# Four quadrants of the array for the state's products, smaller key loads, another order in the joins, and a new table of shifts

## The chip, the core and the metric

The kernel runs on one core of a Trainium2 chip. The time is that of one execution on the device in microseconds (us); of several executions the median is given. TensorE (PE in the rows) has two clock levels, 1.2 and 2.4 GHz; the column PEclk of the rows is the granted clock as a share of the full one.

## What is computed

A recurrent attention with a state that is corrected at each token (the delta rule), for 4 batches of 8 heads with 768 tokens and a head width of 48, and behind it two expert stages on the 3072 tokens of width 384:

```python
k_n = k / (norm(k) + 1e-06)
for t in range(768):
    y[:, :, t] = einsum('bhd,bhde->bhe', q[:, :, t], state)
    v_old = einsum('bhde,bhd->bhe', state, k_n[:, :, t])
    state += b[:, :, t] * einsum('bhd,bhe->bhde', k_n[:, :, t], v[:, :, t] - v_old)
x = y.transpose(0, 2, 1, 3).reshape(3072, 384)
x = ((x @ w1) * (x @ w2) @ w3) @ w_out            # 384 -> 1024 -> 1024 -> 384
lg = x @ phi                                       # 384 -> 32 slots (8 experts of 4)
d = exp(lg - lg.max(0)); d /= d.sum(0) + 1e-09     # softmax over the tokens
slot_out = relu((d.T @ x) @ w1e[e]) @ w2e[e]       # for each expert e
c = exp(lg - lg.max(1)); c /= c.sum(1) + 1e-09     # softmax over the slots
out = c @ slot_out
```

## The kernel before, in words

The tokens go in 24 steps n of 32 tokens. Two steps make a chunk c (12 of them), four steps one solve s (6 of them). Within 32 tokens the recurrence becomes a triangular system for each batch and head, so 32 systems of 32x32 for a step, and a solve inverts those of four steps at once on VectorE (DVE).

- **Keys and queries.** `load(p)` brings the pair p of steps from memory into one of four buffers `kl` (the fourth is called `hold`): rows 64 to 111 and rows 0 to 63, two DMAs on SyncE's queue (L245, L246). `g_step` (L428) multiplies keys with keys ("g", the system's matrix) and keys with queries ("p"); the four first steps do both apart, all later ones together (tiles `gp`). `g_evac` brings the results out: `dg` (L373) on DVE for the solve, `praw`, `kl` (L384, L393, L400, L408) on ScalarE (ACT), GpSimd (POOL) or DVE for the chain.
- **Solves.** `solve_steps(s)`: DVE transposes `dg` to `gl` (L454), normalises the keys by Newton steps on small tiles `sm` (L461 to L482), and eliminates in `xl` (L509, L512; for solve 0 L520, L523). Solves 0 and 1 do two halves of 16x16 and join them: `join` (L525 to L533) multiplies the halves into `xf`, transposes part of it to `xn` (L531) and the whole to `w` (L533), and `join2` (L535) makes the missing quarter on TensorE (`j`, L542, L550) and adds it to `w` (L552). The other solves end in `fin`: a product on POOL (L558) and the transpose to `w` (L560).
- **Chain.** `chain_steps(n)` is one step of the recurrence: `pre` (L585), `ks` (L599: state by keys), `vv` (L610: `w` by values, four copies to `sv`, L575), `yy` (L620: the step's output), at odd n `ss` (L630: keys by new values, added to the state in the two PSUM tiles `sacc`, and copied back), and `xt` (L642: transposes of the output for the next stage).
- **Expert stage.** For each chunk `prod` (L695, tiles `ab`; L699 and L704 bring them out) as three products of the high and low parts, `gtr` (L712), then logits and softmax pieces (L719 to L793), and a tail for the experts (to L1129). The weights are split into high and low parts at the start (`t_w`, `wsl`, `hold`: L290 to L307).

In `ss` each of the 4 batches has 48x48 products, with keys of 64 rows (two steps) for 8 heads. Batches 0 and 1 take rows 0 to 63 and columns 64 to 111 of the array, batches 2 and 3 rows 64 to 127 and columns 0 to 47: two quadrants. A first loop does batches 0 and 2 for all heads, into `sacc0`, a second one 1 and 3, into `sacc1`. The trace records each of these fp32 matmuls twice, 64 records for a chunk.

What sets the order: each step of the program is put into a list `events` with a time (`when`, or `spread` over a range), all in units of a chunk. The times are worked out from constants at the head of the file and, for each label, a number in the table SHIFT. The list is sorted by that time, and the steps issue their instructions in this order; a scheduler then moves instructions within each engine by its own estimate of when their inputs are ready. Each engine runs its own list in order. DMAs of SyncE's queue are in order too.

## Time and profile before

| | us |
|---|---|
| median of 3 executions | 643.93 |
| lowest, highest | 643.07, 649.51 |
| the profiled execution | 642.53 |
| its span in the trace | 640.7 |
| TensorE busy in the span | 548.9 (86%) |
| VectorE busy | 400.3 (62%) |
| ScalarE busy | 278.6 (43%) |
| GpSimd busy | 161.8 (25%) |

Around the span lie 1.8 us that no engine's instruction covers. Busy shares are means over stages with different limits, so the table alone does not tell which engine sets the end.

### The profile page before, as it was taken

The page shows a single profiled execution, that of the slowest core. Times are in us where ns is not written, and L with a number is a line of the kernel's source. Part 1 is how long each engine was busy: PE and PEld are TensorE (multiplying, and loading weights), DVE is VectorE, ACT ScalarE, POOL GpSimd, SP SyncE. Part 2 cuts the span into 40 slices and gives each one's busy share as a digit, 9 for nine tenths or more (in the row PEclk, how much of TensorE's full clock was granted, in tenths as well). Part 3 has the DMA queues.
Part 4 walks back from the last instruction along what each step waited for, and adds up shares of the span by engine and source line. Part 5 has one row for each costly group of instructions (what it writes and reads, how often), then busy time and mean ns, then how long its engine had stood idle before and what let it go on. Part 6 is the DMA issues. An engine that isn't in the chain of part 4 may idle for free.

```text
span 640.7 us, 25996 instructions
## 1 busy us (share of the span) xinstructions
PE 548.9 (86%) x11417; PEld 458.8 (72%) x11417; DVE 400.3 (62%) x1257; ACT 278.6 (43%) x704; POOL 161.8 (25%) x215
## 2 busy tenths in 40 slices
PE   5324546888899799899999999897999999999996
PEld 4323435887777688679888888786989899886464
DVE  3996899998667115994379826997982313134124
ACT  1515644245574436454444455343444454333023
POOL 0726858334254016232030113004010000000100
PEclk9999666598999989999999999999999999999997
DMA  9904234446843720310404030122344130788848
GB/s 205 332 4 146 81 83 144 130 130 204 254 151 129 164 70 17 87 45 18 105 7 96 9 90 30 38 61 63 106 145 155 63 108 2 268 274 318 344 160 265
DMA packets 36945, 81.72 MB, mean 128 GB/s; under 512 B 4352, under 2 KB 17792, under 8 KB 35584
## 3 DMA queue, kind: packets, MB, share of 16 engines
q1 hardware_dynamic: 36832, 80.07, 40.9%
q8 instruction: 89, 1.46, 1.0%
q14 instruction: 24, 0.20, 0.1%
HBM read 69.57 MB, written 10.49 MB: 125 GB/s over the span
## 4 chain that ended last, share of the span: by engine, by line
PE 55%; DVE 26%; issue 6%; DMA 5%; POOL 4%; ACT 3%; SPq 0%; DVEq 0%; POOLq 0%; ACTq 0%
PE ab L695 24%; DMA kl<-kq 4%; PE gp L712 3%; PE yp L620 3%; DVE xl L512 2%; PE vp L610 2%; DVE tmp L509 2%; PE sacc L630 2%; PE gp L428 2%; PE ks L599 2%; PE sacc L1119 2%; PE hp L1098 2%; DVE gl L454 2%; DVE xl L487 1%; PE lp L719 1%
## 5 line engine op out<-in xcount | busy, mean ns | idle before, releaser
L695 PE MATMUL ab<-xT,wsl 128*128 128x256 f32 x1728 | 247.1, 296 | 3.6 <-DVE gT L704 2.2
L695 PEld LDWEIGHTS ab<-xT,wsl 128*128 128x128 f32 x1728 | 221.8, 196 | 15.6 <-issue 6.3
L704 DVE TENSOR_TENSOR gT<-ab,bs 128x256 f32<-128x256 f32 x84 | 35.2, 422 | 87.3 <-ACT bs L699 79.0
L699 ACT COPY bs<-ab 128x256 f32<-128x256 f32 x96 | 35.7, 371 | 68.0 <-PE ab L695 66.3
L585 POOL TENSOR_TENSOR v<-v,nnT 128x384 f32<-128x384 f32 x24 | 21.4, 894 | 139.2 <-DMA v<-vt 57.0
L575 ACT COPY sv<-vp 32x384 f32<-32x384 f32 x96 | 45.1, 470 | 16.2 <-PE vp L610 14.5
L512 DVE TENSOR_TENSOR xl<-xl,tmp 128x84 f32<-128x84 f32 (+35 forms) x220 | 51.5, 266 | 0.7
L509 DVE TENSOR_TENSOR tmp<-xl 128x84 f32<-128x84 f32 (+35 forms) x220 | 49.6, 259 | 0.4
L428 PE MATMUL gp<-kl 48*32 48x64 f32 (+1 forms) x1024 | 35.7, 275 | 11.7 <-ACT kl L408 8.6
L299 POOL TENSOR_TENSOR hold<-hold 128x384 f32<-128x384 f32 (+1 forms) x32 | 32.7, 1025 | 47.9 <-DVE hold L296 23.0
L428 PEld LDWEIGHTS gp<-kl 48*32 48x32 f32 x1024 | 26.1, 121 | 17.8 <-ACT kl L408 8.9
L713 ACT COPY gtok<-gp 128x512 f32<-128x512 f32 x48 | 28.2, 588 | 17.2 <-PE gp L712 15.0
L393 POOL TENSOR_TENSOR kl<-praw,cs 64x256 f32<-64x256 f32 x28 | 25.3, 903 | 33.5 <-ACT praw L384 32.3
L620 PE MATMUL yp<-sv,kl 112*32 112x48 f32 (+2 forms) x1280 | 26.3, 215 | 7.6 <-ACT sv L575 7.6
L291 ACT ACTIVATE hold<-hold,cs 128x384 int32<-128x384 int32 (+1 forms) x32 | 18.7, 589 | 27.7 <-DVE hold L290 27.3
L408 ACT COPY kl<-gp 32x256 f32<-32x256 f32 x64 | 23.2, 363 | 15.0 <-DVE kl L393 11.8
L620 PEld LDWEIGHTS yp<-sv,kl 112*32 112x32 f32 (+2 forms) x1280 | 20.4, 115 | 12.2 <-issue 8.4
L610 PE MATMUL vp<-v,w 32*32 32x48 f32 x1536 | 25.3, 207 | 3.1 <-DVE mst L738 0.9
L646 DVE TENSOR_TENSOR xT<-xp,xT 128x384 fp32r<-128x384 f32 x24 | 13.3, 553 | 22.8 <-ACT xT L645 22.6
L610 PEld LDWEIGHTS vp<-v,w 32*32 32x32 f32 x1536 | 20.1, 107 | 10.2 <-issue 6.0
L712 PE MATMUL gp<-cs,gT 128*128 128x128 f32 x168 | 26.9, 279 | 0.0
L400 POOL TENSOR_TENSOR kl<-praw,cs 32x256 f32<-32x256 f32 x28 | 23.2, 828 | 7.7 <-ACT praw L384 4.8
(248 smaller groups left out, 980.6 us busy)
## 6 DMA issues: line engine op xcount, KB each, us to landing
hold<-w SPq DMA_DIRECT2D x16, 384.0 KB, 3.3
v<-vt SPq DMA_DIRECT2D x24, 192.0 KB, 2.7
kk<-kt SPq DMA_DIRECT2D x12, 384.0 KB, 6.7
unitg<-w1e SPq DMA_DIRECT2D x6, 768.0 KB, 5.7
kl<-kq SPq DMA_DIRECT2D x8, 512.0 KB, 6.8
kl<-kq SPq DMA_DIRECT2D x8, 384.0 KB, 4.6
gx<-w SPq DMA_DIRECT2D x4, 768.0 KB, 8.2
raw_w<-w SPq DMA_DIRECT2D x4, 768.0 KB, 8.8
```

The lines of the kernel that those rows point to most:

```text
L299: G.tensor_tensor(out=w, in0=m, in1=w, op=ALU.mult)
L428: T.matmul(gp[trow(n, b), h - hs[0]], lhsT=t[r, k[j], kc], rhs=t[r, slots, kc], start=True, stop=True)
L509: V.tensor_tensor(out=tmp[:, 0:n, lo:hi], in0=x[:, j + 1:32, j:j + 1].to_broadcast([128, n, hi - lo]), in1=x[:, j:j + 1, lo:hi].to_broadca ...
L512: V.tensor_tensor(out=x[:, j + 1:32, lo:hi], in0=x[:, j + 1:32, lo:hi], in1=tmp[:, 0:n, lo:hi], op=ALU.add)
L575: A.copy(o, i)
L610: T.matmul(p[o, h * D:(h + 1) * D], lhsT=w[o, 8 * n4 + h, :], rhs=r[o, h, :], start=True, stop=True, tile_position=(o.start, o.start))
L620: T.matmul(p[qrow(b), h * D:(h + 1) * D], lhsT=kl[r, (6, 0)[b // 2] if t2 else (4, 2)[b // 2], kcol(h, b)], rhs=sv[r, b, h * D:(h + 1) * D ...
L695: T.matmul(o, lhsT=w[:, m, k], rhs=x[:, k], start=(n == 0), stop=(n == 8))
L699: A.copy(bs, p[:, 256:512])
L704: V.tensor_tensor(out=gt, in0=p[:, 0:256], in1=bs, op=ALU.mult)
L712: T.transpose(p[:, t * 256 + i * 128:t * 256 + (i + 1) * 128], gt[:, t * 128:(t + 1) * 128], ident)
L713: A.copy(gk, p)
```

## The change

1. `ss` goes through the heads once and takes the batches 0, 2, 1, 3 of each. `arow(b)` gives batches 1 and 2 the other columns than before: all four quadrants of the array are used. The copies to `sv` read the rows of `arow`.
2. `load` brings 48 instead of 64 rows for the lower part, except in the first three pairs and pair 5. Rows 48 to 63 are zeros, and stay in the buffer.
3. In solves 0 and 1, POOL's memset of `xf` covers only the two quarters that no product writes, and `join` goes through the halves in the order (16:32), (0:16), each with its own transpose to half of `w`; the transpose to `xn` comes between the last product and the last transpose.
4. Sixteen constants of the order and the table SHIFT are new. It gets labels that it did not have, 'P0' among them (the "p" products of the first four steps), and loses others.

```diff
-DR = 0.3
+DR = 0.306
...
-TW0 = 0.05
-TW1 = 0.8
-CL = 1.0
+TW0 = 0.155
+TW1 = 0.63
+CL = 1.002
...
-GX = 3.912
+GX = 3.584
...
-SHIFT = {'w3': -0.198, ... 'solve4': 0.109, ... 'solve3': 0.122, ...}
+SHIFT = {'w3': -0.205, ... 'solve3': 0.168, ... 'solve2': 0.287, ... 'P0': -0.066, ...}
...
+    def arow(b):
+
+        return srow(b if b % 2 == 0 else 3 - b)
...
-            SP.dma_start(out=t[0:64, 0:4, :], in_=kq[p][0:64])
+
+            n = 64 if p < 3 or p == 5 else 48
+            SP.dma_start(out=t[0:n, 0:4, :], in_=kq[p][0:n])
...
-                G.memset(st["xf"], 0.0)
+                G.memset(st["xf"][:, 0:16, 16:32], 0.0)
+                G.memset(st["xf"][:, 16:32, 0:16], 0.0)
...
-            for r in (slice(0, 16), slice(16, 32)):
+            W[s] = w = px.tile([128, 32, 32], F32, tag="W", name=f"w{s}", bufs=2)
+            for r in (slice(16, 32), slice(0, 16)):
                 V.tensor_tensor(out=xf[:, r, r], in0=x[:, r, r], in1=d[:, r].unsqueeze(2).to_broadcast([128, 16, 16]),
                                 op=ALU.mult)
-            V.transpose(xn.rearrange("p u c -> p c u"), xf[:, :, 0:16].rearrange("p r c -> p c r"))
-            W[s] = w = px.tile([128, 32, 32], F32, tag="W", name=f"w{s}", bufs=2)
-            ends[s] = V.transpose(w[:, :, :].rearrange("p u i -> p i u"), xf)
+                if r.start == 0:
+                    V.transpose(xn.rearrange("p u c -> p c u"), xf[:, :, 0:16].rearrange("p r c -> p c r"))
+                ends[s] = V.transpose(w[:, :, r].rearrange("p u i -> p i u"), xf[:, r, :])
...
-            for h, b in [(h, b) for b2 in range(2) for h in range(H) for b in (b2, b2 + 2)]:
-                r = slice(64 * (b // 2), 64 * (b // 2) + 64)
-                T.matmul(sacc[b % 2][srow(b), h * D:(h + 1) * D], lhsT=k[r, b % 2, h, :],
-                         rhs=sv[r, b, h * D:(h + 1) * D], start=False, stop=(c == NCH - 2),
-                         skip_group_check=True, tile_position=(r.start, 64 - 64 * (b // 2)))
+            for h in range(H):
+                for b in (0, 2, 1, 3):
+
+                    r, o = slice(64 * (b // 2), 64 * (b // 2) + 64), arow(b)
+                    T.matmul(sacc[b % 2][o, h * D:(h + 1) * D], lhsT=k[r, b % 2, h, :],
+                             rhs=sv[r, b, h * D:(h + 1) * D], start=False, stop=(c == NCH - 2),
+                             skip_group_check=True, tile_position=(r.start, o.start))
             for b in (0, 2, 1, 3):
-                copy(n, b, sv[srow(b), b, :], sacc[b % 2][srow(b), 0:384])
+                copy(n, b, sv[srow(b), b, :], sacc[b % 2][arow(b), 0:384])
```

The list of TensorE at the program's start before; g0 to g3 are the "g" products of the first four steps, p0_0 and p0_4 the two halves of the first "p" product, p1_0 and p2_0 those of the next steps:

```order
L428 MATMUL g0_0_147<-kl0_111 32x32 x30
L428 MATMUL g1_0_181<-kl0_111 32x32 x30
L428 MATMUL g2_0_215<-kl1_112 32x32 x32
L428 MATMUL g3_0_249<-kl1_112 32x32 x32
L428 MATMUL p0_0_283<-kl0_111 32x96 x16
L428 MATMUL p0_4_309<-kl0_111 32x96 x16
L428 MATMUL p1_0_335<-kl0_111 32x32 x32
L428 MATMUL p2_0_375<-kl1_112 32x96 x16
```

The same place after the change:

```order
L434 MATMUL g0_0_147<-kl0_111 32x32 x30
L434 MATMUL g1_0_181<-kl0_111 32x32 x30
L434 MATMUL p0_0_215<-kl0_111 32x96 x16
L434 MATMUL g2_0_241<-kl1_112 32x32 x32
L434 MATMUL p0_4_275<-kl0_111 32x96 x16
L434 MATMUL p1_0_301<-kl0_111 32x32 x32
L434 MATMUL g3_0_341<-kl1_112 32x32 x32
L434 MATMUL p2_0_375<-kl1_112 32x96 x16
```

Three "p" products stand ahead of g3 now, one of them ahead of g2; the numbers of records are those of the products times two.

The list of DVE at the join of solve 0 before, from the two products into `xf` to the weights' conversion (`t_w`):

```order
L529 TENSOR_TENSOR xf0_493<-xl0_489,sm0_469 128x16x16 x2
L531 STREAM_TRANSPOSE sums_92<-xf0_493 128x16x32
L533 STREAM_TRANSPOSE w0_555<-xf0_493 128x32x32
L290 TENSOR_SCALAR t_w0_632<-gx_72 128x768
L290 TENSOR_SCALAR t_w1_643<-raw_w1_641 128x768
L292 SCALAR_TENSOR_TENSOR t_w0_632<-gx_72,t_w0_632 128x768
```

The same place after the change, where the first row of `w` is the half 0:16 and the second the half 16:32:

```order
L537 TENSOR_TENSOR xf0_493<-xl0_489,sm0_469 128x16x16 x2
L540 STREAM_TRANSPOSE sums_92<-xf0_493 128x16x32
L541 STREAM_TRANSPOSE w0_553<-xf0_493 128x16x32
L296 TENSOR_SCALAR t_w0_703<-gx_72 128x768
L296 TENSOR_SCALAR t_w1_714<-raw_w1_712 128x768
L541 STREAM_TRANSPOSE w0_553<-xf0_493 128x16x32
L298 SCALAR_TENSOR_TENSOR t_w0_703<-gx_72,t_w0_703 128x768
```

The whole transpose has become two, and two conversions stand between them; the half 16:32, which `join2` reads first, is the last.

The list of DVE at the end of solve 3 before; `hold` and `dg4` are the results of `gp` for the steps 18 and 19, `w3` is the solve's result:

```order
L393 TENSOR_TENSOR hold_114<-gp18_4_5732,cs_90 64x256
L509 TENSOR_TENSOR tmp3_5266<-xl3_5263 128x12
L373 TENSOR_TENSOR dg4_4967<-gp19_0_5779,cs_90 128x256
L400 TENSOR_TENSOR hold_114<-gp19_0_5779,cs_90 32x8x32 x4
L512 TENSOR_TENSOR xl3_5263<-xl3_5263,tmp3_5266 128x12
L704 TENSOR_TENSOR gT5_0_5777<-ab5_1_5912,bs5_1_5931 128x256
L737 TENSOR_REDUCE soft4_5969<-lm4_5873 128x1
L560 STREAM_TRANSPOSE w3_5636<-xf3_5634 128x32x32
L738 TENSOR_TENSOR mst_93<-soft4_5969,mst_93 128x1
L704 TENSOR_TENSOR gT5_2_6069<-ab5_2_6048,bs5_2_6067 128x256
```

The same place after the change:

```order
L519 TENSOR_TENSOR xl3_5231<-xl3_5231,tmp3_5234 128x12
L714 TENSOR_TENSOR gT5_2_5994<-ab5_2_5973,bs5_2_5992 128x256
L568 STREAM_TRANSPOSE w3_5652<-xf3_5650 128x32x32
L747 TENSOR_REDUCE soft4_6004<-lm4_5934 128x1
L748 TENSOR_TENSOR mst_93<-soft4_6004,mst_93 128x1
L749 TENSOR_SCALAR soft4_6004<-mst_93 128x1
L714 TENSOR_TENSOR gT5_2_5994<-ab5_3_6065,bs5_3_6084 128x256
L760 SCALAR_TENSOR_TENSOR zst_94<-zst_94,soft4_6004 128x1
L379 TENSOR_TENSOR dg4_5008<-gp18_4_5796,cs_90 128x128
L399 TENSOR_TENSOR hold_114<-gp18_4_5796,cs_90 64x256 x2
L379 TENSOR_TENSOR dg4_5008<-gp19_0_5842,cs_90 128x256
L406 TENSOR_TENSOR hold_114<-gp19_0_5842,cs_90 32x8x32 x4
```

The evacuations of `gp` for steps 18 and 19 and the L737 (now L747) have moved behind `w3`; the two rows of gT around it have stayed in front.

The list of TensorE at `ss` of chunk 6 before, with the step's output `yp`:

```order
L630 MATMUL sacc0_109<-sv_108,kk6_5640 48x48 x3
L620 MATMUL yp13_6071<-sv_108,kl2_113 32x48 x2
L630 MATMUL sacc0_109<-sv_108,kk6_5640 48x48
L620 MATMUL yp13_6071<-sv_108,kl2_113 32x48 x29
L712 MATMUL gp5_0_6109<-cs_90,gT5_0_5777 128x128 x4
L630 MATMUL sacc0_109<-sv_108,kk6_5640 48x48 x12
L630 MATMUL sacc1_110<-sv_108,kk6_5640 48x48 x16
```

The list of TensorE at `ss` of chunk 9 after the change:

```order
L640 MATMUL sacc0_109<-sv_108,kk9_7617 48x48 x3
L628 MATMUL yp19_8135<-sv_108,hold_114 32x48 x2
L640 MATMUL sacc1_110<-sv_108,kk9_7617 48x48
L628 MATMUL yp19_8135<-sv_108,hold_114 32x48 x29
L640 MATMUL sacc1_110<-sv_108,kk9_7617 48x48
L640 MATMUL sacc0_109<-sv_108,kk9_7617 48x48
L640 MATMUL sacc1_110<-sv_108,kk9_7617 48x48 x2
L640 MATMUL sacc0_109<-sv_108,kk9_7617 48x48 x2
L640 MATMUL sacc1_110<-sv_108,kk9_7617 48x48 x2
```

And that at `ss` of chunk 6 after the change:

```order
L628 MATMUL yp13_6097<-sv_108,kl2_113 32x48
L640 MATMUL sacc0_109<-sv_108,kk6_5637 48x48 x11
L628 MATMUL yp13_6097<-sv_108,kl2_113 32x48 x2
L640 MATMUL sacc1_110<-sv_108,kk6_5637 48x48
L640 MATMUL sacc0_109<-sv_108,kk6_5637 48x48 x3
L628 MATMUL yp13_6097<-sv_108,kl2_113 32x48 x29
L640 MATMUL sacc1_110<-sv_108,kk6_5637 48x48 x13
L640 MATMUL sacc0_109<-sv_108,kk6_5637 48x48 x2
L640 MATMUL sacc1_110<-sv_108,kk6_5637 48x48 x2
```

In chunk 9 pairs for `sacc0` and `sacc1` alternate, as the code is written; in chunk 6 the scheduler has put most of one behind most of the other, so that pairs of two quadrants are next to each other again.

## Rows read from the trace of the kernel before

**Rows 1.** The page's busy time, share of the span and instructions of each engine.

```profile
PE 548.9 (86%) x11417; PEld 458.8 (72%) x11417; DVE 400.3 (62%) x1257; ACT 278.6 (43%) x704; POOL 161.8 (25%) x215
```

**Rows 2.** Busy time by stage: stretch, PE, PEld, DVE, ACT, POOL (instructions), PEclk, DMA share, GB/s.

```profile
0.00:41.00 41.00, 15.26 (x516) 12.04 (x516) 30.62 (x94) 11.31 (x33) 15.72 (x26) 1.00 0.74 211
41.00:102.50 61.50, 29.42 (x969) 24.68 (x970) 50.10 (x64) 32.03 (x64) 39.48 (x25) 0.76 0.27 81
102.50:155.00 52.50, 45.25 (x792) 39.94 (x791) 50.90 (x157) 19.98 (x46) 22.64 (x23) 0.76 0.53 165
...
318.00:366.00 48.00, 45.87 (x945) 40.04 (x944) 42.17 (x168) 21.32 (x55) 7.95 (x20) 1.00 0.17 39
...
436.70:588.00 151.30, 148.08 (x2732) 129.55 (x2732) 67.39 (x254) 65.19 (x168) 12.17 (x25) 1.00 0.44 149
```

**Rows 3.** Timeline of TensorE around `ss` of chunk 5: start, duration, instruction, count, idle before.

```profile
214.03 0.89 PE L620 MATMUL yp<-sv,kl 112*32 112x48 f32 x64
214.84 1.37 PE L630 MATMUL sacc<-sv,kk 64*48 64x48 f32 x52
```

**Rows 4.** DMA queues: packets of the instruction queue, MB, share of 16 engines.

```profile
q8 instruction: 89, 1.46, 1.0%
```

**Rows 5.** Busy time between two stalls of TensorE, columns as in rows 2.

```profile
13.50:22.80 9.30, 3.94 (x127) 3.46 (x127) 7.89 (x20) 3.94 (x12) 3.98 (x6) 1.00 1.03 269
```

**Rows 6.** Timeline of TensorE at the start.

```profile
13.53 0.70 PE L428 MATMUL g<-kl 48*32 48x32 f32 x35 [3.80 <-issue]
...
22.85 3.31 PE L428 MATMUL p<-kl 48*32 48x32 f32 x102 [4.50 <-issue]
```

**Rows 7.** Timeline of DVE: the last `dg` of solve 0.

```profile
14.33 0.42 DVE L373 TENSOR_TENSOR dg<-g,cs 128x256 f32<-128x256 f32 x1 [4.46 <-PE g L428]
```

**Rows 8.** Timeline of DVE in solve 0, two neighbouring pairs.

```profile
34.20 0.87 DVE L520 TENSOR_TENSOR sm<-xl 128x54 f32<-128x54 f32 x2
34.99 0.33 DVE L523 TENSOR_TENSOR xl<-xl,sm 128x54 f32<-128x54 f32 x2
```

**Rows 9.** Timeline of POOL beside them.

```profile
31.79 3.09 POOL L400 TENSOR_TENSOR kl<-praw,cs 32x256 f32<-32x256 f32 x4
```

**Rows 10.** Timeline of DVE: the transpose to `w` of solve 0.

```profile
39.22 1.87 DVE L533 STREAM_TRANSPOSE w<-xf 128x1024 f32<-128x1024 f32 x1
```

**Rows 11.** Timeline of TensorE: the first `j` of the join.

```profile
41.14 1.05 PE L542 MATMUL j<-w,dg 32*32 32x16 f32 x64 [10.98 <-DVE w L533]
```

**Rows 12.** DVE's L307 in 41 to 102.5: count, busy, mean ns, idle before it.

```profile
L307 DVE TENSOR_TENSOR wsl<-t_w,wsl 128x768 fp32r<-128x768 f32 x5 | 6.8, 1357 | 6.3 <-ACT wsl L306 6.3
```

**Rows 13.** Timeline of TensorE at 110.

```profile
113.77 0.61 PE L327 MATMUL wm<-phis,woT 128*128 128x32 f32 x2 [3.88 <-DVE sm L477]
```

**Rows 14.** Timeline of TensorE, 218 to 231.

```profile
218.40 2.40 PE L695 MATMUL ab<-xT,wsl 128*128 128x256 f32 x18
...
224.38 0.45 PE L550 MATMUL j<-t,sums 32*32 32x16 f32 x19 [2.99 <-issue]
...
226.22 4.19 PE L695 MATMUL ab<-xT,wsl 128*128 128x256 f32 x18
```

**Rows 15.** Busy time in 214.9 to 221.9 and 224.4 to 231, columns as in rows 2.

```profile
214.90:221.90 7.00, 5.99 (x188) 5.38 (x186) 0.98 (x2) 3.97 (x9) 0.83 (x1) 1.00 0.85 188
...
224.40:231.00 6.60, 6.60 (x144) 6.30 (x145) 0.51 (x2) 1.22 (x3) 0.00 (x0) 0.53 0.02 5
```

**Rows 16.** Timeline: where solve 3 begins and ends, and who takes its result.

```profile
318.09 1.98 DVE L454 STREAM_TRANSPOSE gl<-dg 128x1024 f32<-128x1024 f32 x1
```

**Rows 17.** The same, at the end of that solve.

```profile
363.89 2.00 DVE L560 STREAM_TRANSPOSE w<-xf 128x1024 f32<-128x1024 f32 x1 [1.38 <-POOL xf L558]
...
366.04 0.66 PE L610 MATMUL vp<-v,w 32*32 32x48 f32 x42 [0.87 <-DVE mst L738]
```

**Rows 18.** DVE by line in 318 to 366: the evacuations into `hold`.

```profile
L393 DVE TENSOR_TENSOR hold<-gp,cs 64x256 f32<-64x256 f32 x4 | 1.7, 416 | 0.1
```

**Rows 19.** DMA issues by line: count, KB each, us from issue to landing.

```profile
kl<-kq SPq DMA_DIRECT2D x8, 512.0 KB, 6.8
```

More of the change, by code (lines that the diff above doesn't have):

```diff
@@ L52 @@
 NL = 4
-J1 = (0.8, 1.2, 1.8, 2.0)
+J1 = (0.82, 1.107, 1.928, 1.875)
 NT12 = 2
@@ L57 @@
 NXT = 6
-GL = (0.35, 0.659, 0.85, 1.06)
+GL = (0.241, 0.657, 0.85, 1.123)
 NX = 6
 NO = 8
-GX = 3.912
+GX = 3.584
 LT = 1.799
-LTS = 0.311
+LTS = 0.351
 JAT = (1, 2, 3)
@@ L66 @@
 LAST = 1
-EA = 11.73
-JO = (-0.7, 0.1, 0.2)
-G1 = -0.341
-S1 = -0.015
-S2 = -0.01
+EA = 11.71
+JO = (-1.075, 0.115, 0.208)
+G1 = -0.294
+S1 = -0.004
+S2 = 0.013
 CA = 224
@@ L82 @@
 WM = (8, 8, 8, 8, 2, 2, 2)
-HT = 2.424
-L3 = -0.04
+HT = 2.423
+L3 = -0.057
 GA = (0.2, -0.09)
@@ L88 @@
 G2 = -0.017
-SA = -0.681
+SA = -0.74
 SB = -0.124
-SHIFT = {'w3': -0.198, 'load8': -0.01, 'solve4': 0.109, 'load6': -0.046, 'load9': -0.004, 'gtr3': 0.007, 'solve3': 0.122, 'prod11': 0.006, 'chain20': 0.021, 'gtr8': -0.158, 'chain17': -0.056, 'gtr6': 0.158, 'post0': -0.014, 'chain19': -0.018, 'gtr10': 0.016, 'back0': 0.257, 'gtr2': -0.016, 'chain13': -0.281, 'gtr9': 0.002, 'back1': 0.128, 'post10': 0.024, 'chain23': 0.001, 'gtr0': -0.012, 'G8': 0.031, 'gtr11': -0.005, 'chain8': 0.006, 'load5': -0.346, 'gtr5': -0.02, 'chain5': -0.257}
+SHIFT = {'w3': -0.205, 'load8': -0.01, 'load9': 0.015, 'solve3': 0.168, 'chain20': 0.021, 'gtr8': 0.095, 'chain17': -0.023, 'gtr6': 0.149, 'chain19': -0.039, 'gtr10': 0.066, 'back0': 0.296, 'chain13': -0.281, 'gtr9': 0.041, 'back1': 0.139, 'post10': 0.105, 'chain23': 0.001, 'gtr0': -0.012, 'G8': 0.031, 'gtr11': -0.005, 'chain8': 0.006, 'load5': -0.346, 'chain5': -0.257, 'prod2': 0.044, 'G18': 0.021, 'chain10': -0.112, 'load11': -0.054, 'gtr4': -0.02, 'post7': -0.027, 'prod3': 0.087, 'load4': -0.057, 'prod5': -0.13, 'post9': 0.119, 'chain11': -0.054, 'chain9': 0.065, 'post2': 0.098, 'chain12': -0.072, 'gtr3': 0.111, 'gtr1': 0.067, 'G4': -0.021, 'back4': -0.073, 'chain16': 0.013, 'gtr5': -0.036, 'chain15': -0.041, 'solve2': 0.287, 'prod8': 0.015, 'back5': -0.061, 'gtr2': -0.045, 'P0': -0.066, 'post1': 0.014, 'G14': -0.037, 'load6': -0.01, 'post11': 0.481, 'prod1': 0.019}
 TRACE = None
```

## The prediction

> **What bounds the kernel now.** I read the busy shares first [rows 1], then the busy time by stage [rows 2], because the mean of 86% for TensorE hides four different limits, and then in each stage the longest idle times of TensorE with what ended them. What the reader is to see:
> - 0 to 41 us: TensorE has 15.26 us of work in 41, DVE 30.62. The chain goes keys, "g" products, `dg`, solve 0 on DVE, `w`.
> - 41 to 155: DVE has 50.10 of 61.50 and then 50.90 of 52.50 (solves and weight conversions). TensorE is also at a mean clock of 0.76.
> - 318 to 366 (and the two like it, before 291.5 and 436.7): TensorE looks full, with 45.87 of 48.00, but it waits at the end for `w`; DVE's chain of solve 3 runs from `gl` at 318.09 [rows 16] to `w` at 363.89 plus 2.00, and `vp` follows at 366.04 after an idle 0.87 [rows 17]. What the trace puts beside that wait (mst) is a neighbour in DVE's list; `w` is the input.
> - 436.7 to 588: 148.08 of 151.30. TensorE is the bound.
>
> So what TensorE saves counts after 436.7 and, in part, in 155 to 318; before 155 and inside solves DVE's order counts.
>
> **The change, part by part.** All is reckoned against the profiled execution, 642.53 us, 1.4 below the median of the runs shown.
>
> *Quadrants.* 52 records of `ss` last 1.37 us, and the last begins some 0.2 before that ends: (1.37 - 0.20) / 51 = 23 ns each. The `yp` just before, which spreads over four column strips, takes (0.89 - 0.20) / 63 = 11 ns each [rows 3]. If four quadrants overlap as four strips do, a chunk saves 64 x 12 ns = 0.77. No row shows two products on the same columns at once, so the bounds are 0 and 11 x 0.77 = 8.5. I take 11 ns, the nearest row. But the new order, shown above, alternates fully only in seven of eleven chunks (2, 4, 5, 7 to 10, roughly); in chunk 6 pairs of two quadrants stand together as before, in 0 too, in 1 and 3 partly. Chunks 5 and 7 lie where `w` is awaited. That leaves chunks 2, 4, 8, 9, 10 whole, 5 x 0.77 = 3.9, and 0.4 of the rest: **-4.3**. The copies begin no later: both accumulators are done at the end of a run half as long, when `sacc0` was done before.
>
> The Trainium skill ("TensorE: Matmul & The Clock Gate", Part 3, "The mechanism") says that a weight load overlaps running products only where its group of rows differs. In the new order every second pair has the same rows as the pair before it on other columns, so by this rule nothing is saved. But `yp` runs at 11 ns with strips that all share rows [rows 3], which speaks against it; it is a rival below.
>
> *Start of the program.* TensorE stalls at 13.53 after 3.80 us and at 22.85 after 4.50, released by "issue", that is by nothing that the engines show [rows 6]. Between the two it does 127 products with their loads [rows 5], 254 instructions; and the whole program's 11417 + 11417 [rows 1] over 89 packets of the instruction queue [rows 4] gives 257 a packet. I conclude that it waits for its own instructions, behind DMAs that fill all 16 engines (share 1.03) [rows 5]. The first boundary lies 219 products into the list (the 35 and 2 after the stall are the rest of g3's 256), the next 127 later, at 346. In the new list p0_0, p0_4 and p1_0 (32 + 32 + 64 records) stand ahead of g3, so g3 begins at record 320, and boundary 346 falls 26 into it. Its last 38 come after the stall that ends at 22.85; `dg`, at 14.33 in before [rows 7], comes at 23.8: +9.4. Given back: solve 0's pairs on DVE take 0.87 us while POOL works and 0.33 just after it stops [rows 8, 9], 0.54 for each. By the two lists POOL has 18 operations beside solve 0 before, some 0.8 us each [rows 9]; a solve that starts 9 us later meets half of them: 9 x 0.54 = -4.8. Net **+4.6**. Bounds: +0.7 (the packet arrives before g3 needs it, since p0_0 now waits for queries first) and +9.4 (nothing given back).
>
> *Joins.* In DVE's new list the half of `w` that `j` needs is the last of the join, behind two conversions and the other half. Before, `j` begins at 41.14, straight after the transpose that starts at 39.22 and takes 1.87 [rows 10, 11]. Two half transposes are 0.93 each by that row; with two conversions between them `j` starts about 1 us later. The two conversions that now precede it, though, are earlier by that half transpose. So in 41 to 102.5, where DVE waits 6.3 us in L307 alone for ACT's casts [rows 12], the new list has the first step of the next weight ahead of the waiting one in four places; I count the waits that are filled so at 2.5 of those 6.3: **-2.5**, bounds +1 and -6.3. The quartered memset of `xf` is on POOL, which has time.
>
> *102.5 to 155.* TensorE waits 3.88 us at 113.77 for a copy (L328) that sits behind Newton steps and a conversion on a full DVE [rows 13]. In the new list L328 follows L704 at once. **-1.5**, bounds 0 and -3.9.
>
> *The stall at 221.* A load of `kl` and what goes with it fill 0.85 of the DMA engines from 214.9 to 221.9 [rows 15]. In it lies a packet boundary of TensorE: idle 2.99 until 224.38, and after it 18 `ab` products take 4.19 instead of 2.40 [rows 14] at a granted 0.53, the lower level (1.2 GHz), for 6.60 us [rows 15]. At the other pace these 6.60 would be 6.60 x 2.40 / 4.19 = 3.8. Cost: 3.0 + 2.8 = 5.8. The new list puts this boundary some 4 us of work later against the load, and the load is 128 KB smaller. I take half, **-3**, bounds 0 and -5.8.
>
> *Key loads.* 512 KB land after 6.8 us [rows 19]; three quarters of the bytes take 1.7 less if it goes by bytes. Most loads come long before their keys are used; I count one in which half of that reaches TensorE: **-1**, bounds 0 and -1.7.
>
> *Solves 2 to 4.* Near the end of solve 3 two L393 at 0.42 [rows 18], four L400 of the same size, and an L737 stand ahead of `w3` in before, and behind it now. 6 x 0.42 = 2.5 off the path that ends in `vp` [rows 17]: **-2.5**; two `dg` moved with them are kept as reserve. TensorE has less to do in the window by two `gtr` steps, so it isn't late itself (45.87 of 48.00 [rows 2]). Solve 2 loses L737 to L739 from its list: **-0.5**. Solve 4's list stays. What is late next is TensorE: with fewer heavy products per packet in steps 12 and 13 a fetch may stall there, **+1.5**, bounds 0 and the 3.0 of 224.38 [rows 14].
>
> Sum: 4.6 - 2.5 - 1.5 - 3 - 1 - 2.5 - 0.5 + 1.5 - 4.3 = -9.2; 642.53 - 9.2 = 633.3. The median of several runs was 1.4 above the profiled one; I add half of that: **634.0 us**. The likeliest case's own range is 630 to 637.5.
>
> **Rivals.**
> - *B, quadrants that share rows don't overlap.* For: the skill's rule, and no row with two products on the same columns. Against: the 11 ns of `yp`. Without 4.3: 638.3.
> - *C, the boundaries fall well.* The stall at 221 goes with its slow clock (-5.8 instead of -3), no stall at steps 12 and 13 (-1.5), L328's gap shrinks by 2.5: 634.0 - 2.8 - 1.5 - 1 = 628.7. For: the boundary lies 4 us of work further from the load. Against: other boundaries move as well.
> - *E, gains before 243 are swallowed.* Solves 2 to 4 start with the evacuation of `gp`, and what TensorE saves before that becomes idle time. Left: +4.6, -2.5 (DVE), -3.0 (solves 2, 3) and -2.3 (chunks 8 to 10): 639.3 + 0.7 = 640.0. For: three stages end in `w`. Against: 155 to 243 is mostly TensorE's.
> - *A, slower: g3 behind the packet.* Price +9.4 with nothing given back, +1.0 for `j`, and later stages that only wait less: only the tail's 2.3 is kept: 642.5 + 10.4 - 2.3 + 0.7 = 651.3. It decides once DVE's pairs beside POOL cost the same as before. Against: the 0.54 between neighbouring pairs [rows 8].
>
> **How the numbers follow.** Forecast 0.46, C 0.20, E 0.18, B 0.10, A 0.06. A measurement of this kernel can tell about 1% from no change: faster means under 637.5, slower above 650.4. Faster: nearly all of the forecast's 0.46, C's 0.20, and 0.03 of B and E, 0.69. Slower: 0.05 of A. The same: 0.26. The range of 8 in 10 reaches from 624, below C by the bounds of the quadrants (8.5 instead of 4.3), to 644, above E: it leaves out A and the far ends.
>
> **What would show it.** Right: `dg` of solve 0 near 23.8 with `g` split by a stall; fewer 0.87 pairs; `sacc` at 11 to 12 ns a record in chunks 8 to 10 and 23 in 6; no idle time with a granted 0.53 near 224; about 45 us from `gl` to `w` in solve 3. Wrong: `dg` still before 17 us; `sacc` at 23 ns everywhere (B); gaps before `vp8`, `vp12` longer by what was saved before (E); a new stall with a slow stretch elsewhere.

## The result and the profile after

The change is slower: 648.98 us (median of 20 executions, 644.56 to 653.09) against 644.27 of before (20 executions, 640.22 to 649.51), a ratio of 1.007 with a 95% interval of 1.0048 to 1.0093. That is under the 1% that the prediction calls a change, but the interval leaves 1 out. Forecast were 634.0, in 624 to 644. Medians here and below are of all executions, ratios and intervals of the fast ones alone (those within 1.5% of the fastest of their kernel), so a ratio is not always the quotient of two medians. The profiled execution of the change took 650.31 us, its span is 648.5 (before 642.53 and 640.7).

The stages, from the starts of the same products in the traces (the first transpose to `w`, the first `vp` product of a step, the first of the last chunk's 144 `ab` products). `vp2` is the `vp` of step 2, and so on; the same holds for `gp18`, `yp11` or `ks13`, and `w3` and `gl3` belong to solve 3. Five traces show the change, two others the kernel before:

| stage | before (2 traces) | change (5 traces) |
|---|---|---|
| start to `w` of solve 0 | 39.2, 40.2 | 43.5 to 44.9 |
| from there to `vp2` | 92.5, 93.4 | 87.1 to 88.2 |
| `vp2` to `vp6` | 111.3, 109.2 | 114.7 to 116.6 |
| `vp6` to `vp11` | 94.3, 94.0 | 91.9 to 92.8 |
| `vp11` to `vp12` | 28.7, 28.7 | 32.1 to 33.2 |
| `vp12` to `vp13` | 7.4, 7.4 | 9.2 to 9.4 |
| `vp13` to `vp16` | 63.3, 63.9 | 64.4 to 67.6 |
| `vp16` to the last `ab` | 117.2, 118.7 | 117.0 to 119.0 |
| from there to the end | 86.8, 86.9 | 85.8 to 85.9 |

Two stretches lose: `vp2` to `vp6`, about 5 us, and `vp11` to `vp16`, 6.4 to 10.7 us (99.4 and 100.0 before, 106.4 to 110.1 after). What the first 40 us lose, the next 90 give back.

First the places that the prediction spoke of. The start, in TensorE's timeline (start, duration, instruction, count, idle before it), then DVE's, against [rows 6, 7]:

```profile
18.33 0.58 PE L434 MATMUL g<-kl 48*32 48x32 f32 x25 [1.32 <-ACT kl L414]
23.35 0.70 PE L434 MATMUL g<-kl 48*32 48x32 f32 x36 [4.44 <-issue]
```
```profile
24.17 0.42 DVE L379 TENSOR_TENSOR dg<-g,cs 128x256 f32<-128x256 f32 x1 [9.74 <-PE g L434]
...
44.46 1.01 DVE L541 STREAM_TRANSPOSE w<-xf 128x512 f32<-128x512 f32 x1
```

g3 is cut after 25 records by the stall that the prediction puts down to instructions, `dg` comes at 24.17 and the first half of `w` at 44.46, 5.2 later than in [rows 10]. Both are near what was forecast (23.8, and +4.6), and what was to be given back is: of the slow pairs on DVE (0.75 us and more) twelve stand in solve 0 before and two after.

The quadrants, in the same timeline at `ss` of chunk 8, against [rows 3]:

```profile
462.13 0.87 PE L628 MATMUL yp<-sv,kl 128*32 128x48 f32 x58
462.92 0.92 PE L640 MATMUL sacc<-sv,kk 64*48 64x48 f32 x56
```

56 records in 0.92 us are (0.92 - 0.20) / 55 = 13 ns each where there were 23: pairs that share rows do overlap. In chunk 6 it is 21 ns still, as forecast.

The stall near 221, against [rows 14]:

```profile
221.99 2.40 PE L705 MATMUL ab<-xT,wsl 128*128 128x256 f32 x18
...
227.70 0.45 PE L558 MATMUL j<-t,sums 32*32 32x16 f32 x18 [2.72 <-issue]
...
229.54 4.19 PE L705 MATMUL ab<-xT,wsl 128*128 128x256 f32 x18
```

It is there as before, with the same slow products behind it. In the second trace of the kernel before, the same boundary waits 1.20 us. And a place of which the prediction said only that the keys would land earlier, `gp18` and what follows, from the timeline of TensorE and the busy time by stretch (length, PE, PEld, DVE, ACT, POOL, granted clock, DMA share, GB/s):

```profile
348.39 0.30 PE L434 MATMUL gp<-hold 48*32 48x128 f32 x2 [0.80 <-DMA hold<-kq]
...
350.71 0.43 PE L434 MATMUL gp<-hold 48*32 48x128 f32 x2 [1.82 <-DMA hold<-kq]
...
352.56 6.59 PE L705 MATMUL ab<-xT,wsl 128*128 128x256 f32 x36
```
```profile
347.00:351.00 4.00, 1.37 (x22) 0.96 (x22) 4.00 (x19) 0.95 (x2) 0.00 (x0) 0.92 0.85 174
351.00:357.00 6.00, 6.00 (x83) 5.85 (x76) 5.03 (x28) 0.20 (x1) 0.00 (x0) 0.50 0.00 0
```

TensorE waits 2.6 us (0.80 and 1.82) for the load of steps 18 and 19, works 1.37 us of four, and then has a granted 0.50, the lower level (1.2 GHz). The same stretch of before:

```profile
350.01 0.96 PE L428 MATMUL gp<-hold 48*32 48x128 f32 x26 [0.72 <-DMA hold<-kq]
...
351.68 2.41 PE L695 MATMUL ab<-xT,wsl 128*128 128x256 f32 x18
```

A wait of 0.72, and 18 products in 2.41 us behind it, the pace of the full clock. SyncE's timeline has the second part of that load, before and after:

```profile
343.45 0.47 SPq L246 DMA_DIRECT2D hold<-kq  x1
```
```profile
343.90 1.07 SPq L252 DMA_DIRECT2D hold<-kq  x1
```

`yp11`, the last reader of the buffer, ends at 343.05 before and at 343.46 after. The load starts right behind it, and with 48 rows this part lands 6.8 us after its issue, with 64 rows 6.5. But 30 `ab` products lie between `yp11` and `gp18` before, and 18 after.

DVE's list shows who pays, in solve 3 after the change:

```profile
321.78 2.06 DVE L460 STREAM_TRANSPOSE gl<-dg 128x1024 f32<-128x1024 f32 x1
...
359.59 0.42 DVE L714 TENSOR_TENSOR gT<-ab,bs 128x256 f32<-128x256 f32 x1 [2.45 <-ACT bs L709]
...
367.22 0.42 DVE L714 TENSOR_TENSOR gT<-ab,bs 128x256 f32<-128x256 f32 x1 [2.56 <-ACT bs L709]
367.56 2.02 DVE L568 STREAM_TRANSPOSE w<-xf 128x1024 f32<-128x1024 f32 x1
```

Two evacuations of `ab` products, late because TensorE was late, stand ahead of the elimination and of the transpose in DVE's list. From `gl` to `w` it takes 45.78 us, as before (45.80 by [rows 16, 17]), though DVE is busy for only 36.6 us of it instead of 40.0. Behind `w`, the moved evacuations are in the way:

```profile
379.08 1.13 PE L607 MATMUL ks<-sv,kl 112*32 112x48 f32 x64 [1.45 <-DVE hold L406]
```

`ks13` waits for the last L406 (L400 before), and from `vp12` to `vp13` it takes 9.4 instead of 7.4.

### The profile page after: what moved, and what is told of

The parts are those of the page before. It is cut to its first block, busy times and chain, and to the rows that moved or that the text cites. A ratio compares the mean times of both kernels' runs of the same rounds, so it can differ in the third digit from the quotient of the medians.

```text
span 648.5 us, 26007 instructions
## 1 busy us (share of the span) xinstructions
PE 551.1 (85%) x11417; PEld 457.2 (70%) x11417; DVE 394.3 (61%) x1259; ACT 280.0 (43%) x704; POOL 161.0 (25%) x217
## 3 DMA queue, kind: packets, MB, share of 16 engines
q1 hardware_dynamic: 36704, 79.02, 40.6%
## 4 chain that ended last, share of the span: by engine, by line
PE 49%; DVE 9%; DMA 6%; POOL 2%; issue 1%; ACT 0%; SPq 0%; POOLq 0%; ACTq 0%; DVEq 0%
PE ab L705 23%; DMA kl<-kq 3%; PE gp L722 3%; PE gp L434 3%; PE yp L628 2%; PE ks L607 2%; PE sacc L1129 2%; PE vp L618 2%; PE lp L729 2%; PE hp L1108 2%; PE sacc L640 1%; PE up L791 1%; DVE tmp L516 1%; DVE xl L519 1%; DMA hold<-kq 1%
## 5 line engine op out<-in xcount | busy, mean ns | idle before, releaser
L714 DVE TENSOR_TENSOR gT<-ab,bs 128x256 f32<-128x256 f32 x84 | 34.7, 419 | 67.6 <-ACT bs L709 54.1
L709 ACT COPY bs<-ab 128x256 f32<-128x256 f32 x96 | 35.8, 373 | 85.8 <-PE ab L705 81.8
L516 DVE TENSOR_TENSOR tmp<-xl 128x84 f32<-128x84 f32 (+35 forms) x220 | 52.2, 270 | 0.5
L519 DVE TENSOR_TENSOR xl<-xl,tmp 128x84 f32<-128x84 f32 (+35 forms) x220 | 48.9, 256 | 0.6
L434 PEld LDWEIGHTS gp<-kl 48*32 48x32 f32 x1024 | 25.5, 119 | 18.1 <-ACT kl L414 8.8
L628 PE MATMUL yp<-sv,kl 112*32 112x48 f32 (+2 forms) x1280 | 28.0, 216 | 6.3 <-ACT sv L583 6.1
L399 POOL TENSOR_TENSOR kl<-praw,cs 64x256 f32<-64x256 f32 x28 | 24.0, 859 | 36.5 <-ACT praw L390 35.3
L656 DVE TENSOR_TENSOR xT<-xp,xT 128x384 fp32r<-128x384 f32 x24 | 13.2, 552 | 30.3 <-ACT xT L655 30.2
L297 ACT ACTIVATE hold<-hold,cs 128x384 int32<-128x384 int32 (+1 forms) x32 | 18.7, 590 | 27.6 <-DVE hold L296 27.5
L618 PEld LDWEIGHTS vp<-v,w 32*32 32x32 f32 x1536 | 20.9, 109 | 11.8 <-DVE v L609 5.0
L414 ACT COPY kl<-gp 32x256 f32<-32x256 f32 x64 | 23.2, 363 | 9.5 <-DVE kl L399 8.6
L406 POOL TENSOR_TENSOR kl<-praw,cs 32x256 f32<-32x256 f32 x28 | 25.0, 893 | 2.1 <-ACT praw L390 0.7
```

What stands on the lines that cost most here:

```text
L434: T.matmul(gp[trow(n, b), h - hs[0]], lhsT=t[r, k[j], kc], rhs=t[r, slots, kc], start=True, stop=True)
L516: V.tensor_tensor(out=tmp[:, 0:n, lo:hi], in0=x[:, j + 1:32, j:j + 1].to_broadcast([128, n, hi - lo]), in1=x[:, j:j + 1, lo:hi].to_broadca ...
L519: V.tensor_tensor(out=x[:, j + 1:32, lo:hi], in0=x[:, j + 1:32, lo:hi], in1=tmp[:, 0:n, lo:hi], op=ALU.add)
L618: T.matmul(p[o, h * D:(h + 1) * D], lhsT=w[o, 8 * n4 + h, :], rhs=r[o, h, :], start=True, stop=True, tile_position=(o.start, o.start))
L628: T.matmul(p[qrow(b), h * D:(h + 1) * D], lhsT=kl[r, (6, 0)[b // 2] if t2 else (4, 2)[b // 2], kcol(h, b)], rhs=sv[r, b, h * D:(h + 1) * D ...
L709: A.copy(bs, p[:, 256:512])
```

## The experiments

T1 names a longer wait for the keys' load near 350, the slow clock behind it and the moved evacuations; T2 the start of the program; T3 the quadrants; T4 to T7 are rivals to single points.

**The change taken apart.** Four kernels on one chip, the kernel before at 643.64.

*Code without the order*: the change's `ss`, `load`, memset and `join`, with the constants and SHIFT of before.

> The change's code (quadrants, 48-row loads, joins in halves) with the constants and the table of before. Theory T1 (the time was lost by the new order in 340 to 390 us: a longer wait for the keys' load of steps 18 and 19, a fall of the granted clock behind it, and the evacuations that now come behind w3; the code itself gains): 2 to 6 us faster than before, sacc records at 13 to 14 ns where pairs alternate, no stretch at a granted 0.50 between 340 and 360, from vp12 to vp13 about 7.4 us. Theory T2 (the time was lost at the start: g3 behind the instruction packet, the join's second half late): also faster, since g3 stays ahead of the p products; dg near 14.3, but j 1 us later behind the join. A third theory T3 (the quadrants themselves bring the stall, since TensorE reaches the keys' load earlier): no faster than before, with a wait of over 1.5 us for the load near 350 and a granted 0.50 behind it.

Measured: 657.03 us, ratio 1.0186 (1.0145 to 1.0227). It is slower than the whole change. T1 and T2 are out on this; T3 has the sign (not faster), not the mechanism: the wait near the load is 1.42 us and no granted 0.50 follows. In its trace (an execution of 651.87, the fastest of six) the loss lies from `vp6` to `vp11`, 100.9 us against 94.3, where TensorE waits 3.64 us for a copy of ACT (L414) ahead of the keys' products. So the code's price depends on the table that it is laid out with.

*Order without the code*: the constants and SHIFT of the change in the kernel before.

> The code of before with the constants and the table of the change. T1: slower than before by 4 to 9 us; a wait for the keys' load near 348 of 1 to 2 us in all (the change's 2.6 less the 0.5 to 0.9 that the quadrants save there), a granted 0.50 behind it, w3 3 to 4 us later against gl3 than DVE's work asks, and 9 us from vp12 to vp13. T2: slower by 4 to 9 us too, but all of it there by 60 us and still there at 214. T3: not slower by more than 2 us, no granted 0.50 in 340 to 360.

Measured: 652.29, ratio 1.0132 (1.0091 to 1.0174). `w` of solve 0 comes at 43.6 and `vp2` at 139.9, 8.1 us later than before, as T2 has it. T1 has the total, but not by its mechanism: there is no wait and no stretch at 0.50 near 350, since in this list 59 `ab` products lie between `yp11` and `gp18`, which TensorE reaches at 358.3, 11 us after the load's buffer is free. T3 is out. From `gl3` to `w` it takes only 40.8 us and from `vp12` to `vp13` 9.9. So the order's saving in solve 3 is real where there is no wait, and larger than forecast; the give-back behind `w` is the order's own. The 5 us that the change wins before `vp2` come of neither half alone: from `w` of solve 0 to `vp2` it takes 96.3 here and 94.1 with the code alone, 92.5 before and 87.1 with both.

*Quadrants alone.*

```diff
-            for h, b in [(h, b) for b2 in range(2) for h in range(H) for b in (b2, b2 + 2)]:
+            for h in range(H):
+                for b in (0, 2, 1, 3):
```

> Before with nothing but the four quadrants. T1: 2 to 5 us faster; 0.5 to 0.9 us less in each chunk's sacc outside solves. T2: the same. T3: within 1 us of before or slower, with the wait near 350 grown by what the sacc of chunk 5 saves and the clock fallen behind it.

Measured: 648.47, ratio 1.0085 (1.0051 to 1.0118), T3's sign. But not by T3's mechanism: the wait near 350 grows to 1.56 us, yet no granted 0.50 follows, and `vp11` to `vp16` takes 99.8, as before. In TensorE's list more than 500 records that are not of `ss` stand elsewhere, above all between 150 and 250 us: the scheduler, given other accumulator rows, lays much of the program out anew. That this new layout costs the 4.8 us is an inference. The edit can't be had without it, and the trace doesn't show the loss: it is of an execution of 644.90, the second fastest of twelve, and no stage is longer than in both traces of before by more than 0.4 us.

*The change without the entry P0.*

> The change without the one entry 'P0' of the table, so that g3 comes ahead of the first p products again. T1: dg of the last step back near 14 us and vp0 3 to 5 us earlier, but at 214 us no more than 1 us of that left and the total within 2 us of the change (647 to 651), with the wait near 348 and the slow stretch still there. T2: 4 to 8 us faster than the change (641 to 645), the gain whole at 214. T3: like T1.

Measured: 647.83, ratio 1.0038 (1.0006 to 1.0071). As T1 has it, `w` of solve 0 is back at 39.95, nothing of that is left at `vp2` (131.99, and 131.55 in the change's first trace), and the wait (0.92 and 1.87) and a slow stretch (0.72 from 354 to 360) are there. The profiled execution is the slowest of the twelve, 652.18. The medians differ by 1 us and the ratios by 0.3%, measured on different chips, so this run alone does not tell T1 from T2.

**The wait for the keys.** Four variants of the change, the kernel before at 644.09.

```diff
-SHIFT = {... 'prod5': -0.13, ...}
+SHIFT = {...}
```

> The change without the entry 'prod5' of the table: in TensorE's list one more group of 18 ab products stands between yp11, whose end lets the keys' load of steps 18 and 19 start, and gp18, which needs it; the evacuations of gp18_4 and gp19 stay behind w3. T1 (a longer wait for that load and the slow clock behind it cost the time): the wait there falls from 2.6 to 0.7 us or less, no granted 0.50 between 345 and 365, and gl3 to w3 takes 43 to 44 us instead of 45.8; the total is 2 to 4 us below the change (645 to 647). T4 (rival: solve 3 on DVE and the moved evacuations set that stretch anyway): the wait and the slow stretch go, but vp12 comes as late after gl3 as in the change, and the total stays within 1 us.

Measured: 648.02, ratio 1.0066 (1.0039 to 1.0092). In the trace all of T1: no wait for these keys, full clock, 100.8 us from `vp11` to `vp16` instead of 107.1, and 40.95 us from `gl3` to `w`:

```profile
324.35 2.06 DVE L460 STREAM_TRANSPOSE gl<-dg 128x1024 f32<-128x1024 f32 x1
...
365.30 1.97 DVE L568 STREAM_TRANSPOSE w<-xf 128x1024 f32<-128x1024 f32 x1
```

36 `ab` products lie between `yp11` and `gp18` now, and `gp18` begins 7.8 us after `yp11` ends, when the load has landed (7.1). The edit is local: TensorE's and DVE's lists differ from the change's hardly anywhere but between 350 and 380 us. Yet the total is only 1 us under the change's, measured elsewhere.

Without 'chain12' as well:

> The change without 'prod5' and 'chain12': gp18 again behind two groups of ab, and the evacuations of gp18_4 (dg4, two of hold) stand ahead of w3 again, those of gp19 behind. T1: as in the run before, and from vp12 to vp13 8 to 8.5 us instead of 9.4 since less of the evacuation stands before ks13 and vp13: 3 to 5 us below the change (644 to 646). T4: the work only moves from one side of w3 to the other, w3 comes 1.1 us later than in the run before and vp13 at the same time; total within 1 us of the change.

Measured: 649.01, ratio 1.0085 (1.0053 to 1.0117). T4 on this point: `vp12` to `vp13` falls from 9.9 to 8.3, but `vp11` to `vp12` grows from 26.5 to 27.6; the work moves from one side of `w3` to the other. A wait of 1.13 us for the keys is back as well.

```diff
-        return srow(b if b % 2 == 0 else 3 - b)
+        return srow(b)
```

> The change with arow giving the old columns, so that the loop over heads and batches is the new one but the products use two quadrants. T5 (what sacc saves reaches the end): sacc 22 to 23 ns a record in chunks 8 to 10, each 0.5 to 0.9 us longer, and the total 2 to 5 us above the change. T6 (rival: behind each sacc TensorE waits for something else, the copies to sv or a product's evacuation, and the saving is lost there): sacc longer by the same, yet from vp16 to the last ab the stretch takes as long as in the change, within 0.5 us, and the total is within 1.5 us.

Measured: 656.36, ratio 1.0208 (1.0176 to 1.024). Its `ss` of chunk 8, to be held against the 0.92 above:

```profile
466.03 1.46 PE L640 MATMUL sacc<-sv,kk 64*48 64x48 f32 x54
```

From `vp16` to the last `ab` it takes 119.05 us, the change's own five traces 117.0 to 119.0; T5's sign, but the total moves by more than `ss` can; this edit lays the list out anew too.

> The change with 64 rows in every key load. T1: the load of steps 18 and 19 lands 0.5 to 1.7 us later after its start, the wait near 350 is longer by as much, and the total 1 to 3 us above the change. T4: landing later but hidden elsewhere; total within 1 us.

Measured: 651.26, ratio 1.0114 (1.0084 to 1.0143), 2 us above the change, on another chip. The load lands 6.9 us after its issue, with 48 rows 6.7 to 7.0 in the five traces of the change, and the wait near 350 is shorter here, not longer (0.83), so T1 is wrong on the load's size. This list is laid out anew from some 90 us on, so the total tells nothing of the load. From `vp11` to `vp13` it takes 37.8 us, 4 us less than the change, and the whole is no faster.

**Is it the execution?** The same kernels again, one execution each, on one more chip.

> The kernel before once more, for a second trace. From vp11 to vp16 99.4 us as in the first trace, within 0.7, with no granted 0.50 between 240 and 600; where the first 240 us differ by over 1 us, that is what one execution differs from the next by.

> The changed kernel once more. T1 (the wait for the keys of steps 18 and 19 and the slow clock behind it are the change's own): a wait of 1.8 to 3 us near 350, a granted 0.50 for 4 to 7 us behind it, and from vp11 to vp16 106 to 107.5 us, against 99.4 of before. T7 (rival: chance of one execution): the wait under 1.5 us, no fall of the clock, and 101 to 104 us from vp11 to vp16.

> As the run before: T1 106 to 107.5 us from vp11 to vp16 with the slow stretch, T7 101 to 104 without it.

> As the run before: T1 106 to 107.5 us from vp11 to vp16 with the slow stretch, T7 101 to 104 without it.

Measured: 644.25 for the kernel before, and 654.27, 652.80 and 653.26 for the change. `vp11` to `vp16` takes 100.0 in the first and 107.7, 106.4, 106.7 in the others, each with waits of 0.84 to 1.02 and 1.76 to 1.83 near 350 and a granted 0.50 of 3.4 to 6.8 us behind them: T1, not chance. Against what was expected, the kernel before had a granted 0.50 too, for 3.4 us at 448.

**The two entries on one chip**, the kernel before at 644.51.

> The changed kernel, timed beside the next two on one chip. T1: median 3 to 7 us above the next one's, and in the trace 106 to 108 us from vp11 to vp16. T4 (what that stretch loses is no loss at the end, or differs by chip): within 1.5 us of the next one.

> The change without 'prod5', on the same chip. T1: 3 to 7 us below the run before, 100 to 102 us from vp11 to vp16, and 2 to 5 us above the kernel before, since the first 340 us of the new order are 2 to 4 us longer. T4: within 1.5 us of the run before.

> The change without 'prod5' and without 'P0': g3 ahead of the p products, gp18 behind two groups of ab. T1: w0 4 us earlier than in the run before, nothing of it left by vp11, and a median within 1.5 us of the run before. T2 (the late start is carried to the end): 3.5 to 5 us below the run before, so level with the kernel before or under it.

Measured: the change 651.98 (1.0113, 1.0066 to 1.0159); without prod5 648.37 (1.0058, 1.0028 to 1.0088); without prod5 and P0 644.23 (0.9993, 0.9963 to 1.0023). The second step is clear of noise. The first is 3.6 us between intervals that overlap; on this chip the change's executions took 650.07 to 653.33 and those without prod5 644.12 to 651.07, and the trace has 6.0 (110.1 to 104.1) from `vp11` to `vp16`, where 100 to 102 was expected. The stretch near 350 without prod5, to be held against the change's above:

```profile
354.59 1.08 PE L434 MATMUL gp<-hold 48*32 48x128 f32 x32
355.60 2.42 PE L705 MATMUL ab<-xT,wsl 128*128 128x256 f32 x18
```
```profile
354.00:360.00 6.00, 6.00 (x81) 4.92 (x80) 5.97 (x30) 1.47 (x4) 0.00 (x0) 1.00 0.05 15
```

So T1 is right on prod5 and T2 on P0, where T1 expected nothing: on this chip the two entries together take all that the change loses, 3.6 and 4.1 of 7.5 us. The share of prod5 is the less certain one. In the twenty executions of the result the change loses only 4.7 us, a ratio of 1.007 against 1.0066 and 1.0058 without prod5; without P0, taking out prod5 as well moves the ratio from 1.0038 to 0.9993 here and 0.9982 below.

**Where P0's part lies, and the next wait of this kind.** The last kernel again, and with `gp22` moved behind more products, on a further chip with the kernel before at 643.72.

> The change without 'prod5' and 'P0' once more, beside the next two. Median within 1% of before (640 to 647). In the trace w0 near 39.5 and all of P0's gain gone by vp2 (131.5 to 133); where the 4 us that P0 cost come back, it is in the stall of 218 to 235, shorter here than 2.2 us or with no slow stretch of over 2 us behind it.

> The run before with the entry 'G22': 0.06 added: four of the first sixteen products of gp22 stay where they are, twelve go behind the next 18 ab. T1: the wait for the keys and the slow stretch behind it (2 to 4 us between vp15 and w4) go in part, 0 to 3 us below the run before. T4: the four that stay wait as long; within 1 us.

> The same with 'G22': 0.1: gp22 wholly behind the next 18 ab and ks16, its evacuation partly behind w4. T1: no wait over 0.5 us for these keys, no granted 0.50 between 410 and 440, vp15 to w4 3 to 4 us shorter than with both, and 1 to 3 us less in the median than in the first of these three runs, which would be under before. T4: what is won there is lost behind w4, as evacuations then stand before ks17 and vp17; within 1 us.

Measured: 643.48 (0.9982, 0.9949 to 1.0015), 643.12 (0.9986, 0.9959 to 1.0013) and 646.82 (1.0041, 1.001 to 1.0073). The last is slower by 3.3 us than the first of the three. P0's lag at the start can't be seen at `vp2` with the change's code: 130.9 to 133.1 with it (eight traces: the change, and those without prod5 or without prod5 and chain12), 131.7 to 133.7 without (five). From `vp2` to `vp6` the kernels differ, 114.7 to 118.0 us with P0 and 107.9 to 112.8 in the four traces without both entries (116.5 in the one without P0 alone, the execution of 652.18).

The lag has gone on in DVE's list. Solve 1 begins 2.4 to 5.2 us later with P0 (`gl` at 110.3 to 111.8 against 106.6 to 107.9) and ends 10 to 13 us later. TensorE then waits for a copy (L334) that stands amid this solve in DVE's list; it ends 0.15 us before the waiting product starts, in both kernels, though the row names a neighbour in one of them. The end of solve 1 and that wait with P0, in the change:

```profile
150.77 1.03 DVE L541 STREAM_TRANSPOSE w<-xf 128x512 f32<-128x512 f32 x1
```
```profile
144.71 0.87 PE L349 MATMUL w3tw<-cs,hold 128*128 128x128 f32 x3 [4.16 <-DVE sm L527]
```

and without both entries:

```profile
138.27 1.98 DVE L541 STREAM_TRANSPOSE w<-xf 128x512 f32<-128x512 f32 x2
```
```profile
142.92 0.52 PE L349 MATMUL w3tw<-cs,hold 128*128 128x128 f32 x3 [2.37 <-DVE mwp L334]
```

The wait is 3.8 to 4.2 us in all eight traces with P0 and at most 2.4 in the four, and `vp3` comes 25.5 to 26.0 us after `vp2` instead of 20.9 to 21.8. Some 1.8 of these 4 us are that wait, and 72 `ab` products lie on the way instead of 64. From `vp3` to `vp5` the kernels with P0 win some 5 us back (48.9 to 52.2 against 53.3 to 57.6), and from `vp5` to `vp6` they lose again (38.8 to 40.6 against 32.9 to 34.2). There lies the stall that the prediction puts down to instructions, 2.2 to 3.3 us with P0, here without it:

```profile
223.23 0.34 PE L558 MATMUL j<-t,sums 32*32 32x16 f32 x19 [1.50 <-issue]
...
224.39 2.40 PE L705 MATMUL ab<-xT,wsl 128*128 128x256 f32 x18
```

1.50 us, and the clock stays up. In its second trace the wait is 1.77, and another stall stands near 170 that none of the eight has:

```profile
172.59 0.57 PE L640 MATMUL sacc<-sv,kk 64*48 64x48 f32 x17 [4.94 <-issue]
```

So the stalls move with the list, as the prediction had it, but what each costs differs by execution: between these two traces of one kernel, 7.7 us apart, 5.5 lie from `vp3` to `vp6`. And taking P0 out does more than put g3 ahead: about 1,080 further records of TensorE and 138 of DVE, between 110 and 240 us, stand elsewhere too. The 4.1 us are the price of the entry with the list that comes of it; how much of it is the late start is not shown.

`gp22` waits as `gp18` did, in the first trace without the two entries:

```profile
417.50 1.75 PE L434 MATMUL gp<-kl 48*32 48x128 f32 x28 [2.25 <-DMA kl<-kq]
419.18 3.26 PE L705 MATMUL ab<-xT,wsl 128*128 128x256 f32 x18
```

and with twelve of its products a group of `ab` later:

```profile
418.80 0.41 PE L434 MATMUL gp<-kl 48*32 48x128 f32 x4 [0.59 <-DMA kl<-kq]
419.14 2.41 PE L705 MATMUL ab<-xT,wsl 128*128 128x256 f32 x18
```

0.59 instead of 2.25 us, and the pace of the full clock. `vp15` to `vp16` falls from 33.0 and 30.2 (two traces) to 28.4, the median by 0.4, which is no difference. Moved wholly, the stretch falls to 27.4 and the next one, to the last `ab`, grows from 117 to 124.1: T4's mechanism, at a higher price than its 1 us. None of these kernels is clearly faster than before.

## Why the prediction was wrong

Some 15 us lie between forecast and measurement. The prediction took solve 3 for a gain of 2.5, where the entry behind it cost up to 3.6: 6 us. The other 9 are gains that did not reach the end: without its +4.6 for the start and its -2.5 for solve 3 the prediction's sum is -11.3, but the kernel without both entries stands level with before (0.9993 and 0.9982).

- **Solves 2 to 4, -2.5: the step that failed.** The evacuations did move behind `w3`, and without the wait solve 3 shortens by 4.9 us (40.95 against 45.80). What the step missed is the other half of the same edit: 'prod5' takes a group of 18 `ab` products out from between `yp11`, which frees the buffer, and `gp18`, which needs its load (30 before, 18 in the change, 36 without the entry). The prediction says of TensorE there that "it isn't late itself", and so put its wait at nothing; it waits 2.6 instead of 0.7 us, runs at half pace for some 6 us, and DVE's list, which has evacuations of these products ahead of the elimination, waits with it. And "off the path that ends in `vp`" forgot the next `vp`: 2.0 us of the 2.5 come back between `vp12` and `vp13`. Together `vp11` to `vp13` loses 6.6 us in the first trace (42.62 against 36.06) where 2.5 were to be won. The sign "about 45 us from `gl` to `w`" came true and told nothing: 45.80 less the forecast 2.5 would have been 43.3. The +1.5 for a new fetch stall is no stall in the first trace, and 0.5 to 1.7 us near 397 in the other four.
- **Key loads, -1.** The price looked at the load's size. The load starts when its buffer is free and TensorE's arrival moves with the order; a wait got longer though fewer bytes came, and the smaller load landed no sooner (6.8 us against 6.5).
- **Start, +4.6, and rival A.** Measured +5.2 at `w`, with the stall inside g3: right in place and size. Carried on to the end as a fixed amount, it was wrong: `vp2` comes no later than before. P0 costs 4.1 us all the same, between `vp2` and `vp6`, where solve 1 ends later and the stall near 225 waits longer; that the number is near 4.6 is luck. Rival A's 651.3 lies nearest to the result by luck too: its premise, nothing given back, is false (`dg` is 9.8 late, `w` 5.2).
- **The stall at 221, -3.** 2.2 to 3.3 us in the five traces, with the same slow `ab` products in the first: 0. The boundary moved as the list told; that a later boundary would wait less was a guess, and fell. The 5.8 us that were to be halved were also those of one execution (1.20 us of wait in the second trace of before).
- **41 to 102.5, -2.5, and 102.5 to 155, -1.5.** From `w` of solve 0 to the first `ab` 62.4 instead of 63.3, so -1.0; the wait for L328 (now L334) is 4.21 instead of 3.88. The first trace wins 5.4 us from `w` to `vp2`, 4.5 of them behind the first `ab`: the sum of the two terms is near, their places are not.
- **Quadrants, -4.3.** The pace was nearly right (13 against 11 ns, from 23: 0.6 us a chunk instead of 0.77), and rival B is out. The gain doesn't show against before: `vp16` to the last `ab` takes as long. Against the new list with two quadrants (118.3 and 119.05, a trace each) most of the change's traces are 1 to 2 us shorter there, so the new order seems to lose what the quadrants win.
- **E** saw rightly that gains before 243 are swallowed (of the 5.4 us that the first trace wins before `vp2`, 3.5 are lost again by `vp6`), but not that a new wait would come; **C** didn't happen.

Still open: how P0's 4 us divide between the late start and the new list (the wait ahead of `vp3` and the stalls are seen, their shares aren't measured apart), why prod5's share of the total differs by chip, and why executions of one kernel lie up to 10 us apart.

## What to carry to other kernels

Where the order lets a transfer start (a buffer's last reader) and takes its result (the first user), count the work that lies between the two in the new list, and hold it against the transfer's time; each product that becomes faster or moves away shortens that cover (here the load had landed 7.2 us after `yp11`; `gp18` came 4.9 us after it, and 7.8 with 18 products more). Price a stall of TensorE with what the clock takes after it, and with the evacuations that stand in another engine's list ahead of the critical work. And where a scheduler lays out the list, an edit's price is not the price of its instructions: the same edits gave ratios of 1.0186 with one table of times and 1.007 with another.

## What had not been expected of the hardware

A wait of 2.6 us in four, with TensorE at work for 1.37 of them, was followed by a granted 0.50 for some 6 us, in which 36 `ab` products took 6.59 us; waits of 0.7, 1.42 and 1.56 at the same place (before, code without order, quadrants alone) were not. Pairs of products that share their rows and differ in their columns run at 13 ns a record, near the 11 of `yp`, against 23 in two quadrants. The second part of the load of steps 18 and 19 landed 6.7 to 7.1 us after its issue with 48 rows, and 6.5 to 6.9 with 64.
